# Local attention in twelve whole-unit steps instead of 24 half-unit steps, with the PSUM banks divided anew

## The chip, the core and the metric

The kernel runs on one core of a Trainium2 chip. The metric is the device time of one execution in microseconds (us). The core's engines are TensorE (PE: matmuls and transposes), VectorE (DVE), ScalarE (ACT), GpSimd (POOL) and SyncE (SP), whose queue issues the transfers. PSUM has eight banks, called `bank0` to `bank7` in the program and `bank_251` to `bank_258` in the lists of instructions below.

## What is computed

```python
scores = scale * np.matmul(q, k.transpose(0, 1, 3, 2))          # B=2, H=8, S=768, D=64
is_global = pos[None, :] < int(n_global)                        # 8
is_local = (rel >= 0) & (rel < int(n_local))                    # 96
scores = scores - slopes * dist
scores = np.where(is_global | is_local, scores, -1000000000.0)
a = softmax(scores)
x = np.matmul(a, v)                                             # rearranged to (1536, 512)
g = x @ w_gate
x = (g * sigmoid(g) * (x @ w_val)) @ w_out                      # d_ff 1536
h = x @ w_in                                                    # d_ff 2048
out = (h * np.cos(h)) @ w_out2
```

The reference has its own names for some of these and writes the softmax out, with a maximum subtracted and 1e-9 added to the sum.

## The kernel before

The 1536 rows of q (two batches of 768) form three chunks of four tiles of 128 rows; with four pairs of heads that makes twelve **units**. A tile of queries sees 240 columns of keys (8 global ones and its local window, with one overlap masked), in two blocks of 120; the first tile of a batch sees only 128 (a narrow tile). Units 0 to 3 have a narrow tile in front, units 4 to 7 have one in third place, units 8 to 11 have none.

`attn_fast` (line 571) runs over half units: a group `g` is two tiles and two heads, 24 groups in all (`NG4`), and one step of the loop at line 703 issues pieces of several groups:

- `S_` (604): four score matmuls into two banks of scores; then for each of four tile-heads, on DVE, scores plus distance with a running minimum (L626), and on ACT the exponential with its sum (L629).
- `R_` and `N_` (633, 638): the reciprocals of the sums on DVE (L636), and on POOL the multiplication of P by them (L642).
- `T_` (645): PE transposes P, tile by tile, into a transpose bank (L654), and the bank is copied to `PT` by ACT or DVE (L660). Which one is decided while the program is built: the one whose planned time `self.t` is less.
- `V_` (662): PE multiplies `PT` with v into the bank of results (L676), which holds a whole unit.
- `X_` (679): when a unit is complete, its result is split into a rounded half on ACT (L400) and the rest on DVE (L404).
- `scale` (592): POOL multiplies a unit's q by the factors of its heads (L595). `load` (576): SP fetches q, k, v of a unit two units ahead.

T and V of a group come three steps behind its S (`LAG`). The order on every engine is that in which the program issues the pieces; engines wait for each other by semaphores. Beside this the program converts the weights of the later layers from 64-bit floats (`work`, line 201): ACT lines 198, 209, 221 and DVE lines 218, 224, 233, 236, 240. A planner (`at`, `bg_fill`) puts these operations into gaps of its own estimate of DVE and ACT, up to a goal that grows with the steps (`READY`). The first three conversions write into the buffers in which unit 0's q, k and v lie (`wr_free`).

Behind the attention come two layers (`mlp1`, `mlp2`), whose matmuls are issued at lines 389 to 391.

The banks are given out in `attention` (786): four for scores, two for transposes, two for results. `PTB` and `PB` are the numbers of buffers for transposed and untransposed P.

Of the kernel before, what the change touches and what calls it, by code (L numbers as in the profile page):

```python
# [54 lines left out]
PTB, PB = 6, 20  # L55

NG4, LAG = 24, 3
# [97 lines left out]
class Body:  # L155
# [415 lines left out]
    def attn_fast(self, p, sc, tr, pv):  # L571
# [4 lines left out]
        def load(u):  # L576
# [3 lines left out]
            v = p.tile([128, 8, 128], F32, tag="v", bufs=4, name="v")  # L580
# [17 lines left out]
        def grp(g):  # L598

            u, tp = divmod(g, 2)  # L600
            c, k = units[u]
            return u, c, k, [(t, *_layout(c)[t]) for t in (2 * tp, 2 * tp + 1)]

        def S_(g):

            u, c, k, tiles = grp(g)
            q, kk, _ = op[u]
            bank = [sc(), sc()]
            self.at("pe", sum(t[2] for t in tiles) / 500, (), [id(b) for b in bank])
            for i, (t, off, w, vb) in enumerate(tiles):  # L610
                for h in range(2):
                    a = slice(64 * h, 64 * h + 64)
                    nc.tensor.matmul(bank[h][:, 256 * i:256 * i + w], lhsT=q[a, 128 * t:128 * t + 128],  # L613
                                     rhs=kk[a, off:off + w], start=True, stop=True)
            sums[g] = p.tile([128, 4], F32, tag="sum", bufs=6, name="sum")
            nmins[g] = p.tile([128, 4], F32, tag="nmin", bufs=6, name="nmin")
            for i, (t, off, w, vb) in enumerate(tiles):
                dist = self.base[:, 0:128] if w == 128 else self.base[:, 128:128 + WW]
                for h in range(2):
                    n = 2 * i + h  # L620
                    pt = p.tile([128, WW], F32, tag="P", bufs=PB, name="P")
                    slope = 2.0 ** -(2 * k + h + 1)
                    nm = nmins[g][:, n:n + 1]

                    self.at("d", w / 700, [id(bank[h])], [("P", g, n)])
                    nc.vector.tensor_tensor_reduce(out=pt[:, :w], in0=bank[h][:, 256 * i:256 * i + w], in1=dist,  # L626
                                                   scale=slope, scalar=3.0e38, op0=ALU.add, op1=ALU.min, accum_out=nm)
                    self.at("a", w / 500, [("P", g, n)], [("P", g, n)])
                    nc.scalar.activation(out=pt[:, :w], in_=pt[:, :w], func=AF.Exp, scale=-1.0, bias=nm,  # L629
                                         accum_out=sums[g][:, n:n + 1])  # L630
                    P[g, n] = pt

        def R_(g):
            self.at("d", 0.35, [("P", g, 3)], [("R", g)])
            nc.vector.tensor_scalar_add(sums[g], sums[g], 1.0e-9)
            nc.vector.reciprocal(sums[g], sums[g])  # L636

        def N_(g):
            for i, (t, off, w, vb) in enumerate(grp(g)[3]):
                for n in (2 * i, 2 * i + 1):  # L640
                    self.at("g", w / 400, [("R", g)], [("P", g, n)])
                    nc.gpsimd.tensor_scalar(out=P[g, n][:, :w], in0=P[g, n][:, :w], scalar1=sums[g][:, n:n + 1],  # L642
                                            scalar2=1.0, op0=ALU.mult, op1=ALU.mult)

        def T_(g):

            for i, (t, off, w, vb) in enumerate(grp(g)[3]):
                bank = tr()
                nk, nb = (128, 1) if w == 128 else (KB, 2)
                self.at("pe", 0.11 * 2 * nb, [("P", g, 2 * i), ("P", g, 2 * i + 1)], [id(bank)])  # L650
                for h in range(2):
                    for j in range(nb):
                        o = 128 * (nb * h + j)
                        nc.tensor.transpose(bank[:nk, o:o + 128], P[g, 2 * i + h][:, nk * j:nk * j + nk], self.ident)  # L654
                    del P[g, 2 * i + h]
                pt = ptb[g, i] = p.tile([128, 512], F32, tag="PT", bufs=PTB, name="PT")

                e = "a" if self.t["a"] <= self.t["d"] else "d"
                self.at(e, 0.16 + nb * 0.21, [id(bank)], [("E", g, i)])
                (nc.scalar.copy if e == "a" else nc.vector.tensor_copy)(pt[:nk, :256 * nb], bank[:nk, :256 * nb])  # L660

        def V_(g):

            u, c, k, tiles = grp(g)
            v = op[u][2]
            if g % 2 == 0:
                pvb[u] = pv()
            self.at("pe", 0.25 * sum(len(t[3]) for t in tiles), [("E", g, 0), ("E", g, 1)], [id(pvb[u])])
            for i, (t, off, w, vb) in enumerate(tiles):
                nk = 128 if w == 128 else KB  # L670
                pt = ptb.pop((g, i))
                for j, bl in enumerate(vb):
                    for h in range(2):
                        a = slice(64 * h, 64 * h + 64)
                        o = 128 * (len(vb) * h + j)
                        nc.tensor.matmul(pvb[u][a, 128 * t:128 * t + 128], lhsT=v[:nk, bl, a], rhs=pt[:nk, o:o + 128],  # L676
                                         start=j == 0, stop=j == len(vb) - 1)

        def X_(g):

            u, c, k, _ = grp(g)
            if g % 2 == 0:
                return lambda: None
            xt, ps = self.xtile(c, k), pvb.pop(u)
            self.x[c].append(xt)
            self.split_hi(xt, ps)
            return lambda: self.split_lo(xt, ps)
# [238 lines left out]
```

## Time and profile before

| | |
|---|---|
| median of three runs | 654.55 us (654.12 to 655.04) |
| the profiled execution | 653.59 us |
| its span in the profile | 651.8 us |
| PE busy over the span | 632.7 us (97%) |
| DVE, ACT, POOL busy | 436.1, 391.8, 56.4 us |
| first score matmul of the attention | 9.72 us |
| first matmul of the MLP | 90.70 us |

The span begins with the first and ends with the last instruction that the profile shows; the profiled execution takes 1.8 us more than it. Busy times are sums over an engine's instructions; a busy PE is not PE at its peak, since the ends of matmuls are modelled. The chain that ended last is made of MLP matmuls (lines 389 to 391) for 84% of the span.

### The profile page before, as it was taken

To read this page: it belongs to the slowest core of one execution; us is meant where nothing else is said; L and a number is where in the kernel's file an instruction comes from. 1 tells how busy PE (TensorE), PEld (TensorE's weight loads), DVE (VectorE), ACT (ScalarE), POOL (GpSimd) and SP (SyncE) were. 2 spreads that over 40 slices of the span, in tenths; PEclk is the share of its full clock that TensorE was granted. 3 is DMA by queue.
4 is the path that set the end of the run, shared out by engine and by line. 5 is a ranking of instruction groups with operands and counts; after the bars stand their busy time and mean duration, and the time that the engine had idled before them with its cause. 6 is when DMAs were issued, how large, how long until landed. Compare 5 with 4: busy or idle time off the path is not lost.

```text
span 651.8 us, 8771 instructions
## 1 busy us (share of the span) xinstructions
PE 632.7 (97%) x3176; PEld 516.0 (79%) x3176; DVE 436.1 (67%) x770; ACT 391.8 (60%) x670; POOL 56.4 (9%) x112
## 2 busy tenths in 40 slices
PE   5999989999999999999999999999999999999996
PEld 3776768888888888888888888888888888888885
DVE  4899978877777766438888647866454444544443
ACT  4888776555555544435566349877666666666662
POOL 2677630000000000000000000000000000000000
PEclk9899999999999999999999999999999999999999
DMA  7865246555555455555876643330010000010001
GB/s 259 321 204 199 103 140 227 204 191 200 190 189 196 164 206 195 209 178 193 291 272 240 220 140 98 105 97 25 1 65 1 1 1 1 24 41 0 2 1 69
DMA packets 22803, 88.96 MB, mean 136 GB/s; under 512 B 2656, under 2 KB 4192, under 8 KB 18400
## 3 DMA queue, kind: packets, MB, share of 16 engines
q1 hardware_dynamic: 22320, 88.06, 38.9%
q8 instruction: 27, 0.44, 0.3%
q10 hardware_dynamic: 432, 0.26, 0.1%
q14 instruction: 24, 0.20, 0.1%
HBM read 67.34 MB, written 20.97 MB: 135 GB/s over the span
## 4 chain that ended last, share of the span: by engine, by line
PE 91%; DVE 4%; DMA 2%; issue 0%; ACT 0%; DVEq 0%
PE bank L389 28%; PE bank L391 28%; PE bank L390 28%; PE bank L676 3%; PE bank L613 2%; PE bank L654 2%; DVE P L626 2%; DMA kk<-in_kw 2%; DVE PT L660 1%; DVE x L404 0%; DVE wr L218 0%; DVE sum L636 0%; DVE wr L240 0%; DVE w L224 0%; ACT w L209 0%
## 5 line engine op out<-in xcount | busy, mean ns | idle before, releaser
L389 PE MATMUL bank<-x,w 128*128 128x512 f32 x336 | 131.0, 390 | 0.0
L391 PE MATMUL bank<-x,w 128*128 128x512 f32 x336 | 130.8, 389 | 0.0
L390 PE MATMUL bank<-x,w 128*128 128x512 f32 x336 | 130.8, 389 | 0.0
L481 DVE SCALAR_TENSOR_TENSOR u<-r,bank 128x512 f32<-128x512 f32 x48 | 33.0, 688 | 80.2 <-ACT r L479 80.2
L391 PEld LDWEIGHTS bank<-x,w 128*128 128x128 f32 x336 | 63.1, 188 | 13.1
L389 PEld LDWEIGHTS bank<-x,w 128*128 128x128 f32 x336 | 63.1, 188 | 13.1 <-issue 0.2
L390 PEld LDWEIGHTS bank<-x,w 128*128 128x128 f32 x336 | 63.1, 188 | 13.0
L478 ACT ACTIVATE r<-bank,cst 128x512 f32<-128x512 f32 x48 | 33.0, 687 | 46.0 <-PE bank L391 46.0
L198 ACT ACTIVATE wr<-r 128x1024 f32<-128x1024 f32 x34 | 39.0, 1147 | 29.1 <-DMA r<-in_win 11.7
L391 PE MATMUL bank<-t,w 128*128 128x512 f32 x144 | 56.1, 390 | 0.0
L389 PE MATMUL bank<-t,w 128*128 128x512 f32 x144 | 56.1, 389 | 0.0
L390 PE MATMUL bank<-t,w 128*128 128x512 f32 x144 | 56.1, 389 | 0.0
L629 ACT ACTIVATE P<-P,nmin 128x240 f32<-128x240 f32 (+1 forms) x96 | 44.8, 469 | 13.4 <-DVE nmin L626 13.4
L491 DVE TENSOR_TENSOR r<-bank,r 128x512 f32<-128x512 f32 x48 | 33.1, 689 | 28.4 <-ACT r L490 28.4
L489 ACT ACTIVATE r<-r 128x512 f32<-128x512 f32 x48 | 30.4, 633 | 33.8 <-DVE r L482 33.6
L642 POOL TENSOR_SCALAR P<-P,sum 128x240 f32<-128x240 f32 (+1 forms) x96 | 48.1, 519 | 21.7 <-DVE sum L636 7.8
L425 ACT ACTIVATE e<-bank 128x512 f32<-128x512 f32 x36 | 21.4, 595 | 46.0 <-PE bank L391 44.3
L391 PE MATMUL bank<-big,g 128*128 128x512 f32 x120 | 46.8, 390 | 0.0
L389 PE MATMUL bank<-big,g 128*128 128x512 f32 x120 | 46.7, 390 | 0.0
L390 PE MATMUL bank<-x,big 128*128 128x512 f32 x120 | 46.7, 389 | 0.0
L390 PE MATMUL bank<-big,g 128*128 128x512 f32 x120 | 46.7, 389 | 0.0
L389 PE MATMUL bank<-x,big 128*128 128x512 f32 x120 | 46.7, 389 | 0.0
(95 smaller groups left out, 1237.0 us busy)
## 6 DMA issues: line engine op xcount, KB each, us to landing
scr<-wr SPq DMA_DIRECT2D x34, 512.0 KB, 2.9
r<-in_wo SPq DMA_DIRECT2D x14, 1024.0 KB, 5.8
r<-in_gv SPq DMA_DIRECT2D x12, 1024.0 KB, 5.9
wl<-scr SPq DMA_DIRECT2D x18, 512.0 KB, 5.0
r<-in_win SPq DMA_DIRECT2D x8, 1024.0 KB, 6.0
wr<-scr SPq DMA_DIRECT2D x16, 512.0 KB, 3.4
v<-in_vw SPq DMA_DIRECT2D x11, 512.0 KB, 5.5
out<-wr SPq DMA_DIRECT2D x11, 256.0 KB, 2.4
```

Source lines behind the costliest of these rows:

```text
L198: self.nc.scalar.activation(out=w, in_=self.raw[n][:, :, 1].bitcast(F32), func=AF.Abs)
L389: mm(out, lhsT=ah, rhs=bh, start=first, stop=False)
L390: mm(out, lhsT=ah, rhs=bl, start=False, stop=False)
L391: mm(out, lhsT=al, rhs=bh, start=False, stop=last)
L425: nc.scalar.activation(out=tmp, in_=ps[0], func=AF.Silu)
L478: nc.scalar.activation(out=r, in_=h, func=AF.Identity, scale=INV2PI, bias=self.magic)
L481: nc.vector.scalar_tensor_tensor(out=u, in0=r, scalar=-C1, in1=h, op0=ALU.mult, op1=ALU.add)
L489: nc.scalar.activation(out=r, in_=r, func=AF.Abs)
L491: nc.vector.tensor_tensor(out=r, in0=h, in1=r, op=ALU.mult)
L629: nc.scalar.activation(out=pt[:, :w], in_=pt[:, :w], func=AF.Exp, scale=-1.0, bias=nm, accum_out=sums[g][:, n:n + 1])
L642: nc.gpsimd.tensor_scalar(out=P[g, n][:, :w], in0=P[g, n][:, :w], scalar1=sums[g][:, n:n + 1], scalar2=1.0, op0=ALU.mult, op1=ALU.mult)
L676: nc.tensor.matmul(pvb[u][a, 128 * t:128 * t + 128], lhsT=v[:nk, bl, a], rhs=pt[:nk, o:o + 128], start=j == 0, stop=j == len(vb) - 1)
```

## The change

A step now issues pieces of whole units: four tiles and two heads, eight score matmuls into all four banks of scores. There are twelve steps (`NU`) and T and V lag two of them. Three banks serve the transposes, and one the results. A unit's reciprocals and normalisations are issued in two halves (`R_(u, i)`): the first behind the S of the unit, the second among the DVE operations of the next unit's S. `scale` and `load` are called once a step, `X_` as one piece at a step's start. v has five buffers for four, PT eight for six, P 24 for 20. `wr_free` is raised a step earlier or later by the new count of steps, and the goal grows with the new steps.

```diff
-PTB, PB = 6, 20
+PTB, PB = 8, 24
-NG4, LAG = 24, 3
+NU, LAG = 12, 2
...
-        def S_(g):
-            u, c, k, tiles = grp(g)
-            bank = [sc(), sc()]
+        def S_(u):
+            c, k, tiles = grp(u)
+            bank = [[sc(), sc()] for _ in range(2)]
+            for i in range(2):
+                self.at("pe", sum(t[2] for t in tiles[2 * i:2 * i + 2]) / 560, (), [id(b) for b in bank[i]])
+                for t, off, w, vb in tiles[2 * i:2 * i + 2]:
+                    for h in range(2):
+                        a = slice(64 * h, 64 * h + 64)
+                        nc.tensor.matmul(bank[i][h][:, 256 * (t % 2):256 * (t % 2) + w],
+                                         lhsT=q[a, 128 * t:128 * t + 128], rhs=kk[a, off:off + w],
+                                         start=True, stop=True)
+            for t, off, w, vb in tiles:
+                if t == 2 and u:
+                    R_(u - 1, 1)
...
+        def R_(u, i):
+            self.at("d", 0.35, [("P", u, 4 * i + 3)], [("R", u, i)])
+            h = sums[u][:, 4 * i:4 * i + 4]
+            nc.vector.tensor_scalar_add(h, h, 1.0e-9)
+            nc.vector.reciprocal(h, h)
+            for t, off, w, vb in grp(u)[2][2 * i:2 * i + 2]:
+                for n in (2 * t, 2 * t + 1):
+                    self.at("g", w / 400, [("R", u, i)], [("P", u, n)])
+                    nc.gpsimd.tensor_scalar(out=P[u, n][:, :w], in0=P[u, n][:, :w], scalar1=sums[u][:, n:n + 1],
...
-        def T_(g):
-            for i, (t, off, w, vb) in enumerate(grp(g)[3]):
+        def T_(u):
+            for t, off, w, vb in grp(u)[2]:
                 bank = tr()
...
-        for s in range(NG4 + LAG + 1):
-            self.wr_free = 3 if s > 1 + LAG else 2 if s > 1 else 0
-            low = X_(s - LAG - 1) if s > LAG else None
-            if LAG <= s < NG4 + LAG:
+        for s in range(NU + LAG + 1):
+            self.wr_free = 3 if s > LAG else 2 if s > 0 else 0
+            if s > LAG:
+                X_(s - LAG - 1)
+            if LAG <= s < NU + LAG:
                 T_(s - LAG)
-            if s < NG4:
-                if s % 2 == 1 and s // 2 + 1 < len(units):
-                    scale(s // 2 + 1)
+            if s < NU:
+                if s + 1 < len(units):
+                    scale(s + 1)
                 S_(s)
-            if 1 <= s <= NG4:
-                R_(s - 1)
-                N_(s - 1)
-            if low:
-                low()
-            if LAG <= s < NG4 + LAG:
+                R_(s, 0)
+            elif s == NU:
+                R_(s - 1, 1)
+            if LAG <= s < NU + LAG:
                 V_(s - LAG)
-            if s % 2 == 0 and s // 2 + 2 < len(units):
-                load(s // 2 + 2)
+            if s + 2 < len(units):
+                load(s + 2)
             yield s
...
-        for s in self.attn_fast(p, Rot([banks[i] for i in (0, 1, 6, 7)]), Rot(banks[2:4]), Rot(banks[4:6])):
-            self.filling, self.goal = True, READY * s / NG4
+        for s in self.attn_fast(p, Rot([banks[i] for i in (0, 1, 6, 7)]), Rot(banks[2:5]), Rot(banks[5:6])):
+            self.filling, self.goal = True, READY * s / NU
```

The lists below are the instructions of one engine in the order of the program. First ACT in the attention's second half, where the units are wide: `P` rows are exponentials, `x` rows the rounded half of the split, `PT` rows copies out of transpose banks, `wr` a weight conversion. Before:

```order
L629 ACTIVATE P,sum<-P,nmin 128x240 x8
L400 CAST x_1184<-bank_256 128x512
L629 ACTIVATE P,sum<-P,nmin 128x240 x4
L660 COPY PT<-bank_254 120x512
L629 ACTIVATE P,sum<-P,nmin 128x240 x4
L400 CAST x_1276<-bank_255 128x512
L629 ACTIVATE P,sum<-P,nmin 128x240 x4
L660 COPY PT<-bank_254 120x512
```

With the change:

```order
L634 ACTIVATE P,sum<-P,nmin 128x240 x8
L400 CAST x_1097<-bank_256 128x512
L665 COPY PT<-bank_254 120x512
L665 COPY PT<-bank_255 120x512
L665 COPY PT<-bank_254 120x512
L198 ACTIVATE wr_84<-r_817 128x1024
L634 ACTIVATE P,sum<-P,nmin 128x240 x8
L400 CAST x_1193<-bank_256 128x512
```

The exponentials of a whole unit now stand in a row, and a split and three of a unit's four copies stand behind them; in the same stretch of the list before there is one copy or split to four exponentials.

PE in the same part of the program: `P` rows are transposes into a transpose bank, `kk` rows scores, `PT` rows results. Before:

```order
L676 MATMUL bank_255<-PT,v 64x128 x8
L654 MATMUL bank_253<-cst,P 120x128 x4
L654 MATMUL bank_254<-cst,P 120x128 x4
L613 MATMUL bank_252<-kk,q 128x240
L613 MATMUL bank_257<-kk,q 128x240
L613 MATMUL bank_252<-kk,q 128x240
L613 MATMUL bank_257<-kk,q 128x240
L676 MATMUL bank_255<-PT,v 64x128 x8
```

With the change:

```order
L679 MATMUL bank_256<-PT,v 64x128 x16
L659 MATMUL bank_253<-cst,P 120x128 x4
L659 MATMUL bank_254<-cst,P 120x128 x4
L659 MATMUL bank_255<-cst,P 120x128 x4
L659 MATMUL bank_253<-cst,P 120x128 x4
L615 MATMUL bank_252<-kk,q 128x240
L615 MATMUL bank_257<-kk,q 128x240
```

A unit's four tiles now go through three banks in a row: the fourth writes the bank of the first (253 here), and the scores stand behind it.

POOL at the start of the program: `wr_82` is the q of unit 0, the `q` rows are the scalings of units 1 and 2, `P` rows normalisations. Before:

```order
L595 TENSOR_SCALAR wr_82<-wr_82,cst 128x512
L595 TENSOR_SCALAR q<-q,cst 128x512
L642 TENSOR_SCALAR P<-P,sum 128x128 x2
L642 TENSOR_SCALAR P<-P,sum 128x240 x6
L595 TENSOR_SCALAR q<-q,cst 128x512
```

With the change:

```order
L595 TENSOR_SCALAR wr_82<-wr_82,cst 128x512
L595 TENSOR_SCALAR q<-q,cst 128x512
L647 TENSOR_SCALAR P<-P,sum 128x128 x2
L647 TENSOR_SCALAR P<-P,sum 128x240 x2
L595 TENSOR_SCALAR q<-q,cst 128x512
L647 TENSOR_SCALAR P<-P,sum 128x240 x4
```

The scaling of unit 2 has moved ahead of the second four normalisations of unit 0.

## Rows read from the trace of the kernel before

**Rows 1.** Windows: us; busy of PE, PEld, DVE, ACT, POOL; PEclk; DMA share; GB/s.
```profile
20.20:75.60 55.40, 53.14 (x534) 38.83 (x534) 52.79 (x222) 45.74 (x163) 39.78 (x81) 1.00 0.63 214
...
90.70:640.00 549.30, 549.30 (x2425) 455.09 (x2424) 356.61 (x458) 323.19 (x442) 0.00 (x0) 1.00 0.36 127
```

**Rows 2.** Timeline of PE: start us, us, engine, line, operation, out<-in, shapes.
```profile
14.02 1.66 PE L654 MATMUL bank<-cst,P 128*128 128x128 f32 x6 [1.25 <-POOL P L642]
...
20.24 0.90 PE L613 MATMUL bank<-kk,q 64*128 64x128 f32 x8 [0.16 <-DMA kk<-in_kw]
...
66.37 1.08 PE L613 MATMUL bank<-kk,q 64*128 64x240 f32 x8
67.38 1.09 PE L676 MATMUL bank<-PT,v 120*64 120x128 f32 x16
68.41 1.09 PE L654 MATMUL bank<-cst,P 128*120 128x128 f32 x8
69.43 1.08 PE L613 MATMUL bank<-kk,q 64*128 64x240 f32 x8
...
75.61 1.08 PE L613 MATMUL bank<-kk,q 64*128 64x240 f32 x8
...
89.54 1.23 PE L676 MATMUL bank<-PT,v 120*64 120x128 f32 x16 [0.28 <-ACT PT L660]
90.70 0.50 PE L389 MATMUL bank<-x,w 128*128 128x512 f32 x1
```

**Rows 3.** Timeline of DVE, the same columns: first minimum operations of a step.
```profile
21.14 0.29 DVE L626 CUSTOM_DVE_ANT_0 P<-bank,base 128x128 f32<-128x128 f32 x1 [0.33 <-PE bank L613]
...
70.65 0.41 DVE L626 CUSTOM_DVE_ANT_0 P<-bank,base 128x240 f32<-128x240 f32 x1 [0.19 <-PE bank L613]
```

**Rows 4.** Timeline of ACT: exponentials, a split, a conversion, a copy.
```profile
21.48 0.40 ACT L629 ACTIVATE P<-P,nmin 128x128 f32<-128x128 f32 x1 [1.02 <-DVE nmin L626]
...
23.22 0.56 ACT L400 CAST x<-bank 128x512 fp32r<-128x512 f32 x1
...
23.69 1.18 ACT L221 ACTIVATE se<-r 128x1024 int32<-128x1024 uint32 x1
...
24.75 0.51 ACT L629 ACTIVATE P<-P,nmin 128x240 f32<-128x240 f32 x1
...
71.10 0.49 ACT L629 ACTIVATE P<-P,nmin 128x240 f32<-128x240 f32 x1 [0.57 <-DVE nmin L626]
...
88.91 0.58 ACT L660 COPY PT<-bank 120x512 f32<-120x512 f32 x1
```

**Rows 5.** Groups by shape, 9 to 91 us: count | busy us, mean ns | idle.
```profile
L629 ACT ACTIVATE P<-P,nmin 128x240 f32<-128x240 f32 x80 | 38.5, 484 | 8.6 <-DVE nmin L626 8.6
...
L660 DVE COPY PT<-bank 120x512 f32<-120x512 f32 x31 | 20.6, 681 | 2.1 <-PE bank L654 2.0
...
L629 ACT ACTIVATE P<-P,nmin 128x128 f32<-128x128 f32 x16 | 6.3, 394 | 4.8 <-DVE nmin L626 4.8
...
L660 ACT COPY PT<-bank 120x512 f32<-120x512 f32 x9 | 5.1, 572 | 0.6 <-PE bank L654 0.6
...
L236 DVE SCALAR_TENSOR_TENSOR wr<-r,wr 128x1024 int32<-128x1024 int32 x2 | 2.4, 1222 | 0.0
...
L660 ACT COPY PT<-bank 128x256 f32<-128x256 f32 x3 | 1.0, 348 | 0.0
```

**Rows 6.** Timeline of POOL: normalisations and a scaling.
```profile
15.59 1.78 POOL L642 TENSOR_SCALAR P<-P,sum 128x240 f32<-128x240 f32 x4 [0.40 <-ACT P L629]
19.38 0.69 POOL L595 TENSOR_SCALAR q<-q,cst 128x512 f32<-128x512 f32 x1 [2.01 <-DMA q<-in_qT]
...
78.72 3.00 POOL L642 TENSOR_SCALAR P<-P,sum 128x240 f32<-128x240 f32 x4 [0.98 <-PE bank L654]
```

**Rows 7.** Windows of a microsecond at the start, columns as in rows 1.
```profile
13.00:14.00 1.00, 0.00 (x0) 0.00 (x0) 0.97 (x9) 1.00 (x5) 0.41 (x2) 1.00 1.02 381
...
17.00:18.00 1.00, 1.00 (x12) 1.00 (x12) 1.00 (x7) 0.60 (x3) 0.37 (x1) 0.50 1.00 400
```

More of the change, by code (lines that the diff above doesn't have):

```diff
@@ L596, in scale, with grp @@
                                     op0=ALU.mult, op1=ALU.mult)
-        def grp(g):
-            u, tp = divmod(g, 2)
+        def grp(u):
             c, k = units[u]
-            return u, c, k, [(t, *_layout(c)[t]) for t in (2 * tp, 2 * tp + 1)]
-        def S_(g):
-            u, c, k, tiles = grp(g)
+            return c, k, [(t, *_layout(c)[t]) for t in range(4)]
+        def S_(u):
+            c, k, tiles = grp(u)
             q, kk, _ = op[u]
-            bank = [sc(), sc()]
[L609 to L617, printed above, removed]
+            bank = [[sc(), sc()] for _ in range(2)]
+            sums[u] = p.tile([128, 8], F32, tag="sum", bufs=4, name="sum")
+            nmins[u] = p.tile([128, 8], F32, tag="nmin", bufs=4, name="nmin")
+            for i in range(2):
[9 more added lines that the diff above has]
+                    R_(u - 1, 1)
@@ L631, in S_ @@
[L631 to L638, printed above, removed]
-            for i, (t, off, w, vb) in enumerate(grp(g)[3]):
-                for n in (2 * i, 2 * i + 1):
-                    self.at("g", w / 400, [("R", g)], [("P", g, n)])
-                    nc.gpsimd.tensor_scalar(out=P[g, n][:, :w], in0=P[g, n][:, :w], scalar1=sums[g][:, n:n + 1],
+                                         accum_out=sums[u][:, n:n + 1])
@@ L653, in T_, with V_ @@
                         o = 128 * (nb * h + j)
-                        nc.tensor.transpose(bank[:nk, o:o + 128], P[g, 2 * i + h][:, nk * j:nk * j + nk], self.ident)
-                    del P[g, 2 * i + h]
-                pt = ptb[g, i] = p.tile([128, 512], F32, tag="PT", bufs=PTB, name="PT")
+                        nc.tensor.transpose(bank[:nk, o:o + 128], P[u, 2 * t + h][:, nk * j:nk * j + nk], self.ident)
+                    del P[u, 2 * t + h]
+                pt = ptb[u, t] = p.tile([128, 512], F32, tag="PT", bufs=PTB, name="PT")
                 e = "a" if self.t["a"] <= self.t["d"] else "d"
-                self.at(e, 0.16 + nb * 0.21, [id(bank)], [("E", g, i)])
+                self.at(e, 0.16 + nb * 0.21, [id(bank)], [("E", u, t)])
                 (nc.scalar.copy if e == "a" else nc.vector.tensor_copy)(pt[:nk, :256 * nb], bank[:nk, :256 * nb])
-        def V_(g):
-            u, c, k, tiles = grp(g)
+        def V_(u):
             v = op[u][2]
[L666 to L669, printed above, removed]
+            out = pvb[u] = pv()
+            for t, off, w, vb in grp(u)[2]:
+                self.at("pe", 0.22 * len(vb), [("E", u, t)], [id(out)])
                 nk = 128 if w == 128 else KB
-                pt = ptb.pop((g, i))
+                pt = ptb.pop((u, t))
                 for j, bl in enumerate(vb):
@@ L675, in V_, with X_ @@
                         o = 128 * (len(vb) * h + j)
[L676 removed]
+                        nc.tensor.matmul(out[a, 128 * t:128 * t + 128], lhsT=v[:nk, bl, a], rhs=pt[:nk, o:o + 128],
                                          start=j == 0, stop=j == len(vb) - 1)
[L679 to L684, printed above, removed]
+        def X_(u):
+            c, k = units[u]
+            xt = self.xtile(c, k)
             self.x[c].append(xt)
[L686 to L687 removed]
+            self.split_out(xt, pvb.pop(u))
         op[0] = self.pro.q, self.pro.k, self.pro.v
```

18 lines of the change are left out of this document (9 added, 9 removed).

## The prediction

> **What bounds the kernel now.** I read the windows first. From 90.70 us on TensorE (PE) is busy for all 549.30 us of the window that ends at 640 [rows 1]; nothing there waits, and the change touches no line that runs there. So the end moves by as much as the first MLP matmul, now at 90.70 us, moves [rows 2]. The attention is the part ahead of it. Between the first score matmul of unit 2 (20.24 us) and that of unit 11 (75.61 us) PE is busy 53.14 of 55.40 us and VectorE (DVE) 52.79, ScalarE (ACT) 45.74 [rows 1]: PE and DVE are both nearly full, ACT has a sixth free. The PE timeline shows the undisturbed pattern: scores, results and transposes of half a unit take 1.01, 1.03 and 1.02 us, so 3.06 us a half step, 6.1 a unit [rows 2].
>
> I call a step's pieces as the code does: S the eight score matmuls, T the transposes (tile 0 to 3), V the results, X the two halves of the split. E0 to E3 are the copies of the four transposed tiles out of their banks.
>
> **The copies move to ACT.** Before, ACT's queue mixes one split or one copy with each four exponentials, and most copies are DVE's. In the changed order ACT has, in every step from the fourth on, eight exponentials, then the split of the unit three steps back, then E0, E1 and E3; DVE has E2 alone. DVE is relieved by more than 20 copies, which I cost at nothing: it no longer sets the pace. PE meanwhile has three transpose banks for four tiles. Tile 3 writes the bank of tile 0, so it waits for E0; S of the unit follows tile 3 in PE's queue; and E0 stands on ACT behind the exponentials of the previous unit. That closes a ring of waits, which I price for one step, from S(k) to S(k+1), all four tiles wide:
>
> - S starting to the first bias-and-minimum on DVE: 70.65 - 69.43 = 1.22 us, DVE idle until PE released it [rows 2, 3].
> - that one to the first exponential: 71.10 - 70.65 = 0.45 [rows 3, 4].
> - eight exponentials of 0.48 each, back to back: 3.84 [rows 5].
> - the split, 23.22 to 23.69: 0.47 [rows 4].
> - E0: 0.57 [rows 5], and 0.05 to PE, as the copy that starts at 88.91 and takes 0.58 lets V go at 89.54 [rows 2, 4]: 0.62.
> - tile 3's transposes, half of 69.43 - 68.41: 0.51 [rows 2].
>
> The sum is 7.11 us, against 6.1 of PE work: PE idles a microsecond in each step. E1, E3 and a background conversion fit into the time in which ACT waits for the next scores.
>
> Units whose first tile is narrow (0 to 3) have 21.14 - 20.24 = 0.90 and 21.48 - 21.14 = 0.34 at the start [rows 2, 3], six exponentials of 0.48 and two of 0.39 (3.66), and a narrow E0 of 0.35 + 0.05 [rows 5]: 6.28. Units 4 to 7 have their narrow tile third: 1.67 + 3.66 + 0.47 + 0.62 + 0.51 = 6.93, but 6.71 from S(4) to S(5), since that E0 is unit 3's. From S(2) to S(11) that is 2 x 6.28 + 6.71 + 3 x 6.93 + 3 x 7.11 = 61.4 us. Before it is 55.37 [rows 2]. **Loop: +6.0.**
>
> **Background work in the loop.** An ACT conversion steps 24.75 - 23.69 = 1.06 us [rows 4]; E3 is over 0.6 us after S has started and the first exponential comes 1.67 after it, so it just fits: nothing. If that gap were missed, it costs 1.06 at each of seven places, which I keep for the upper end. On DVE a step's list in the ring is the second half of the split, E2, and the first minimum, which the scores release at 7.11 + 1.22 = 8.3 us after the previous S. The first half of the split is over at 6.0; the second half and E2 take 0.68 each [rows 5], to 7.4; a conversion of 1.22 behind them [rows 5] makes that 8.6, 0.3 too late. This stands once in the changed list, in step 9, with two more conversions ahead of the split, so I take 0.4; one more stands among the minimum operations of step 4, where the exponentials have used up less than its length by then: 0.3. **+0.7** (between 0, all in slack, and 2.4, two at full length).
>
> **The start.** GpSimd (POOL) scales q of unit 2 when its transfer lands, at 19.38 us, having waited for it [rows 6]. Before, all eight normalisations of unit 0 stand ahead of that scaling and are done by 17.37. Now only four do: the scaling moves ahead of the other four, which start at 19.38 + 0.69 = 20.07 and take 1.78, to 21.85. Transposes of tiles 2 and 3 of unit 0 wait for them, and S(2) behind those starts at 21.85 + 0.05 + 0.25 = 22.15, not 20.24. SP's queue has the same transfers in the same order here, so q lands when it did. **+1.9** (0 if q lands earlier, 3 if later). Unit 3's scaling is past that: no wait stands in front of it before, and its transfer is issued as early.
>
> PE then does nothing from about 15.6, where the first two tiles' transposes give way to the next piece now [rows 2], to 20.6 us. In the run before the granted clock was 0.50 (1.2 GHz) from 17 to 18, after a stretch with PE at 0.00 busy from 13 to 14 [rows 7]. I expect the lower level behind the longer gap too: tile 3's last transposes, the first scores and the results of unit 0 take up to twice as long, of which the ring sees some **+0.4** (0 to 1.5).
>
> **The end.** Behind S(11) the last exponential is over at 1.67 + 3.84 = 5.51, E0 of unit 10 at 6.55, tile 3 at 7.11, V(10) at 9.15. The last normalisations come behind a DVE copy, at 7.7, and beside a two-operand conversion take 3.00, as at 78.72 [rows 6]: 10.8. Tile 3 of unit 11 follows to 11.3, V(11) to 13.35. Before it was 90.70 - 75.61 = 15.09 [rows 2]. **-1.7** (-3 to 0).
>
> **Nothing** I cost: the wider sums and minima buffers; the fifth v and the 24 P buffers, whose readers are two steps back; one result bank instead of two, since T and S of a step lie between the split that reads it and the V that writes it again. The later release of the third scratch buffer and the planner's new goal leave DVE's list at the last split a few conversions further on than before, so the first MLP weights are no later. If they were late, PE would wait in the MLP; nothing there is idle now.
>
> **Sum:** 1.9 + 0.4 + 6.0 + 0.7 - 1.7 = +7.3 us on the profiled execution's 653.59, so 660.9. That execution is 0.96 under the median of the three runs, 654.55; I leave the number as the sum gives it, and the range covers that difference.
>
> **Rivals.**
>
> *The copies are hidden (faster).* Three banks let tiles 0 to 2 go while E0 runs. If E0 ended before tile 2's transposes do, PE would never wait and a step would be its work. In a step tile 2 ends 2.03 (S) + 2.04 (V) + 1.53 = 5.6 us after the previous S; E0 ends at 1.67 + 3.84 + 0.47 + 0.57 = 6.55. It decides only if eight exponentials took under 2.9 us, 0.36 each, where rows show 0.48 [rows 5], or if ACT's list were taken out of order. PE's own work from S(2) to S(11), with the narrow tiles, is 50.6 us: 55.4 - 50.6 = -4.8, with the start's +1.9 and the end's -1.7 this is 649.0. The Trainium skill, "Perfetto Trace Analysis", section "Optimizing Tensor Performance", says that independent matmul groups should rotate through banks so that the evacuation of one overlaps the next group's matmuls. By that rule a third transpose bank gives this rival's time; against it stands what occupies ACT in the rows. 5%.
>
> *Only start and end change.* The ring is there, but its extra microsecond a step lies in waits that the loop has already (DVE's 95% share speaks for some of that): +1.9 + 0.4 - 1.7, 654.2. Before has PE idle only 2.3 us in the loop, which speaks against it. 4%.
>
> *The conversions do not fit.* E3 waits for tile 3, so a conversion can push the exponentials by its whole length: 7 x 1.06 = 7.4 more, 668.3. ACT waits 0.57 us before its first exponential in the row at 71.10, less than a conversion [rows 4]. 8%.
>
> **How the numbers follow.** The ring has 83%. Its own terms, with the ends above, go from 657 to 665. The range goes to 656 and 666: below lie the hidden copies and the start-and-end case (9%), above the conversions (8%), so little more than 17% is out. A measurement can tell about 0.2% here, 1.3 us: faster 6% (the first rival and a little), same 4%, slower 90%.
>
> **What would show it.** S matmuls of units 8 to 11 start 7.1 us apart, not 6.1. The idle time before the transposes is put down to ACT's PT copy, in a gap of about 1 us once a step; ACT busy over 90% in the loop and DVE under 85%. S(2) starts near 22 us, behind transposes that wait for POOL, and POOL for the transfer of q. The first MLP matmul comes near 98 us and the stretch behind it stays 549 us. Wrong would be: steps of 6.1 us and no idle time before tile 3 (then the evacuation is hidden), S(2) still at 20.2, or new waits in the MLP.

## The result, and the profile after

The changed kernel takes 663.94 us (median of four runs, 662.83 to 664.11) against 654.66 us for the kernel before on the same chip: 1.0139 times as long, with a 95% interval of 1.0126 to 1.0152. The prediction was 660.9 us in a range of 656 to 666, with a chance of 0.90 for slower. The profiled execution took 663.83 us, 10.24 more than that of before.

The windows of the changed kernel, columns as in [rows 1], cut where its stages now end: up to the scores of unit 2, the loop to those of unit 11, the end of the attention, the MLP.

```profile
9.95:23.05 13.10, 8.06 (x47) 5.35 (x46) 7.63 (x42) 8.39 (x33) 4.93 (x12) 0.81 0.99 384
23.05:87.63 64.58, 52.37 (x531) 42.80 (x531) 47.88 (x207) 56.76 (x185) 43.72 (x84) 0.93 0.56 189
87.63:100.92 13.29, 11.83 (x146) 10.01 (x145) 10.79 (x32) 11.91 (x28) 7.07 (x12) 1.00 0.02 4
100.92:650.20 549.28, 549.28 (x2425) 454.85 (x2424) 354.35 (x455) 321.37 (x441) 0.00 (x0) 1.00 0.36 125
```

The MLP is untouched: 549.28 us, PE busy throughout, against 549.30 [rows 1]. It starts 10.22 us later (100.92 for 90.70), and this is all of the difference: start +2.81 (23.05 for 20.24), loop +9.21 (64.58 for 55.37), end -1.80 (13.29 for 15.09) [rows 2]. In the loop PE's busy time hardly changed and DVE's fell by 5 us, but ACT's rose by 11 and the loop grew around it.

PE's timeline, columns as in [rows 2]: the start, the last two steps of the loop (scores of units 9, 10 and 11), the first MLP matmul.

```profile
21.12 2.00 PE L659 MATMUL bank<-cst,P 128*120 128x128 f32 x8 [4.67 <-POOL P L647]
23.05 2.53 PE L615 MATMUL bank<-kk,q 64*128 64x128 f32 x16
...
72.37 3.43 PE L615 MATMUL bank<-kk,q 64*128 64x240 f32 x16
...
79.82 0.62 PE L659 MATMUL bank<-cst,P 128*120 128x128 f32 x4 [0.78 <-POOL P L647]
80.37 1.89 PE L615 MATMUL bank<-kk,q 64*128 64x240 f32 x16
...
87.08 0.62 PE L659 MATMUL bank<-cst,P 128*120 128x128 f32 x4 [1.46 <-POOL P L647]
87.63 1.89 PE L615 MATMUL bank<-kk,q 64*128 64x240 f32 x16
...
100.92 0.50 PE L389 MATMUL bank<-x,w 128*128 128x512 f32 x1
```

DVE and then ACT in the same steps: the conversion and the first minimum of step 9, the first minimum of step 10; on ACT the first and last of step 10's exponentials, then the split, E0 and E1 in one row, E3, and behind it a conversion and the next exponential.

```profile
72.32 1.35 DVE L236 SCALAR_TENSOR_TENSOR wr<-r,wr 128x1024 int32<-128x1024 int32 x1
74.34 0.41 DVE L631 CUSTOM_DVE_ANT_0 P<-bank,base 128x240 f32<-128x240 f32 x1 [0.67 <-PE bank L615]
...
81.59 0.41 DVE L631 CUSTOM_DVE_ANT_0 P<-bank,base 128x240 f32<-128x240 f32 x1 [1.08 <-PE bank L615]
```

```profile
82.04 0.50 ACT L634 ACTIVATE P<-P,nmin 128x240 f32<-128x240 f32 x1 [0.93 <-DVE nmin L631]
...
85.41 0.48 ACT L634 ACTIVATE P<-P,nmin 128x240 f32<-128x240 f32 x1
...
85.89 0.56 ACT L400 CAST x<-bank 128x512 fp32r<-128x512 f32 x1
86.35 1.06 ACT L665 COPY PT<-bank 120x512 f32<-120x512 f32 x2
87.79 0.58 ACT L665 COPY PT<-bank 120x512 f32<-120x512 f32 x1 [0.38 <-PE bank L659]
88.27 1.05 ACT L209 CAST w<-wr 128x1024 fp32r<-128x1024 f32 x1
89.30 0.50 ACT L634 ACTIVATE P<-P,nmin 128x240 f32<-128x240 f32 x1
```

The ring can be read off piece by piece from 80.37 to 87.63: scores to first minimum 1.22, to the first exponential 0.45, eight exponentials 3.85, the split 0.46, E0's start to tile 3 0.73, tile 3 to the next scores 0.55. That is the whole 7.26 us of a step. But the row of tile 3 names POOL's normalisation as its releaser, and so does most of this wait in the list of waits from 23 to 90 us (engine and line, what it waited for: us in total, times, longest):

```profile
PE bank L659 <- POOL P L647: 7.8, 6, 1.9
...
PE bank L659 <- ACT PT L665: 4.4, 3, 1.9
```

Tile 3 waits for two things, its own normalised P and the bank that E0 empties. POOL's timeline, up to the tile 3 that starts at 87.08:

```profile
83.45 3.56 POOL L647 TENSOR_SCALAR P<-P,sum 128x240 f32<-128x240 f32 x8 [2.08 <-DVE sum L643]
```

By the program's order the first four of these eight are unit 9's and the last four unit 10's, and this tile 3 is unit 9's. Its normalisations were over half way through the row, at 85.2, while E0, 0.58 long, was over at 86.93, 0.15 before tile 3. The label goes by POOL's last event ahead of that start, the end of the row at 87.01, which is unit 10's. Counted in the same way, tile 3 follows the end of E0 by 0.14 or 0.15 us in all nine steps of the loop, and in eight of them its own P had been ready for 1.5 to 2.0 us (in the step that ends with the scores of unit 5 for 0.08). The experiments test this. **Theory A** is the prediction's: the copy of tile 0, behind the exponentials and the split in ACT's queue. **Theory B** is the label's: POOL.

### The profile page after: what moved, and what is told of

Its sections match the earlier page's. It is cut to its first block, busy times and chain, and to the rows that moved or that the text cites. A ratio compares the mean times of both kernels' runs of the same rounds, so it can differ in the third digit from the quotient of the medians.

```text
span 662.0 us, 8783 instructions
## 1 busy us (share of the span) xinstructions
PE 631.1 (95%) x3176; PEld 519.9 (79%) x3176; DVE 426.0 (64%) x748; ACT 401.5 (61%) x692; POOL 57.1 (9%) x112
## 4 chain that ended last, share of the span: by engine, by line
PE 92%; ACT 2%; POOL 2%; issue 2%; DVE 1%; DVEq 1%; POOLq 0%; ACTq 0%
PE bank L391 28%; PE bank L389 28%; PE bank L390 28%; PE bank L615 3%; PE bank L659 2%; PE bank L679 2%; POOL P L647 2%; ACT P L634 2%; DVEq L845 1%; DVE P L631 1%; PE bank L698 1%; ACT PT L665 0%; ACT x L400 0%; ACT w L209 0%; DVEq L853 0%
## 5 line engine op out<-in xcount | busy, mean ns | idle before, releaser
L391 PE MATMUL bank<-big,g 128*128 128x512 f32 x120 | 46.8, 390 | 0.0
L389 PE MATMUL bank<-big,g 128*128 128x512 f32 x120 | 46.7, 389 | 0.0
L389 PE MATMUL bank<-x,big 128*128 128x512 f32 x120 | 46.7, 389 | 0.0
L390 PE MATMUL bank<-x,big 128*128 128x512 f32 x120 | 46.7, 389 | 0.0
L391 PE MATMUL bank<-x,big 128*128 128x512 f32 x120 | 46.7, 389 | 0.0
```

The source lines that it names most:

```text
L389: mm(out, lhsT=ah, rhs=bh, start=first, stop=False)
L390: mm(out, lhsT=ah, rhs=bl, start=False, stop=False)
L391: mm(out, lhsT=al, rhs=bh, start=False, stop=last)
```

## The experiments

Ratios are to the kernel before, run on the same chip beside each.

**1. The split out of the ring.** X is called between tile 0's transposes and tile 1's; each copy keeps its engine.

```diff
-        def T_(u):
+        def T_(u, mid=lambda: None):
...
             for t, off, w, vb in grp(u)[2]:
+                if t == 1:
+                    mid()
                 bank = tr()
...
-                e = "a" if self.t["a"] <= self.t["d"] else "d"
+                e = "d" if t == 2 or (u == 0 and t < 2) else "a"
...
-            if s > LAG:
-                X_(s - LAG - 1)
+            mid = (lambda: X_(s - LAG - 1)) if s > LAG else (lambda: None)
...
-                T_(s - LAG)
+                T_(s - LAG, mid)
```

> The changed kernel with the split of the next results called between the transposes of tile 0 and those of tile 1, so that ScalarE's order in each step is exps, copy of tile 0, split half, copies of tiles 1 and 3, while every copy stays on the engine that it has in the changed kernel. Theory A (ScalarE's copy of tile 0, which stands behind all exps and the split half, opens the bank that tile 3 needs): the split half of 0.47 us leaves the loop in each of nine steps, so the spacing of the scores falls from 7.26 to about 6.8 us and the time from 663.9 to about 659.7 us (658.5 to 661). Theory B (the last event of that wait, POOL's normalisation, is what tile 3 waits for): POOL's work stands where it stood, spacing 7.26, time 663.5 to 664.5 us.

Measured: 661.3 us, 1.0109 (1.0092 to 1.0126). PE's timeline, two quiet steps, and DVE's in a later one:

```profile
42.43 1.71 PE L615 MATMUL bank<-kk,q 64*128 64x240 f32 x16
...
49.04 1.71 PE L615 MATMUL bank<-kk,q 64*128 64x240 f32 x16
...
55.63 1.71 PE L615 MATMUL bank<-kk,q 64*128 64x240 f32 x16
```

```profile
77.21 1.28 DVE L236 SCALAR_TENSOR_TENSOR wr<-r,wr 128x1024 int32<-128x1024 int32 x1
...
79.62 0.39 DVE L631 CUSTOM_DVE_ANT_0 P<-bank,base 128x240 f32<-128x240 f32 x1
```

Steps of 6.61 and 6.59 us, where the changed kernel has 7.09 and 7.08: the split's 0.47 has left the ring, as A says, and B's "no change" is wrong. The time fell by less than expected, because three later steps were long (7.32, 7.68 and 7.75 us). In the last, scores that started at 77.41 got their first minimum 2.21 us later instead of 1.22, behind a conversion, the split's second half and a copy on DVE; the step of 7.68 had its scores at half speed (3.24 us at 62.95). The time lies 0.3 us above A's range.

**2. The copy of tile 0 made later.** E0 and E2 change engines; on DVE E0 stands behind the split's second half.

```diff
-                e = "a" if self.t["a"] <= self.t["d"] else "d"
+                e = "d" if t == 0 else "a"
```

> The changed kernel with one edit: the copy of tile 0 goes to VectorE, that of tile 2 to ScalarE; the split stays ahead of the transposes, so the copy of tile 0 stands on VectorE behind the split's second half, which itself waits for ScalarE's first half. Theory A: the copy comes later by the second half (about 0.84 us) in each of nine steps, so the spacing goes from 7.26 to about 8.1 us and the time to about 671 us (668 to 673). Theory B (POOL's normalisation is what tile 3 waits for): 663 to 665 us.

Measured: 674.85 us, 1.0312 (1.0295 to 1.0329). PE's timeline:

```profile
62.08 1.71 PE L615 MATMUL bank<-kk,q 64*128 64x240 f32 x16
...
69.44 0.62 PE L659 MATMUL bank<-cst,P 128*120 128x128 f32 x4 [2.73 <-DVE PT L665]
69.99 3.51 PE L615 MATMUL bank<-kk,q 64*128 64x240 f32 x16
```

A step of 7.91 us, 0.80 more than the same one in the changed kernel, and the wait is now put down to the copy on DVE; POOL's work is what it was. A holds for the step, and moving the copy to another queue is no gain by itself. The time is 1.9 us above A's range: three steps with scores at half speed, the one shown at 69.99 us among them, took 8.4 to 8.9 us.

**3. The copy of tile 0 made early.** E0 and E2 on DVE, and the split's second half behind the copies.

```diff
-                e = "a" if self.t["a"] <= self.t["d"] else "d"
+                e = "d" if t % 2 == 0 else "a"
...
-            self.split_out(xt, pvb.pop(u))
+            ps = pvb.pop(u)
+            self.split_hi(xt, ps)
+            return lambda: self.split_lo(xt, ps)
...
-            if s > LAG:
-                X_(s - LAG - 1)
+            low = X_(s - LAG - 1) if s > LAG else None
             if LAG <= s < NU + LAG:
                 T_(s - LAG)
+            if low:
+                low()
```

> The changed kernel with the copy of tile 0 (and of tile 2) on VectorE and the split's second half behind all copies on that engine, the first half ahead of them on ScalarE as before: the copy that opens tile 3's bank now stands behind no exp at all. Theory A: the wait of tile 3 goes, TensorE's work of 6.1 us becomes the bound of a wide step, the loop falls from 64.6 to 55 to 57 us and the time to 654.5 to 656.5 us. Theory B (POOL's normalisation): the normalisations stand where they stood and the time stays at 663 to 665 us. A third way, that ScalarE's own work per step is the bound (88% busy in the loop), would leave 6.4 us a step or more and a time of 657 us or more.

Measured: 658.71 us, 1.0066 (1.0049 to 1.0083). PE's timeline:

```profile
67.32 1.89 PE L615 MATMUL bank<-kk,q 64*128 64x240 f32 x16
...
72.72 0.62 PE L659 MATMUL bank<-cst,P 128*120 128x128 f32 x4 [0.37 <-POOL P L647]
73.27 1.89 PE L615 MATMUL bank<-kk,q 64*128 64x240 f32 x16
...
88.11 3.61 PE L679 MATMUL bank<-PT,v 120*64 120x128 f32 x32 [1.64 <-DVE x L404]
```

The step is 5.95 us, the next and last one too, and the loop 56.56, inside A's 55 to 57: with E0 behind no exponential the ring is gone. (The other steps took 5.3 to 7.2 us, the longest with its scores at half speed. Tile 3 still follows E0, now by DVE's queue, with 0.37 us of idle time here.) The time, 658.71, is above A's range. It lies where the third way put it, but that way's step of 6.4 us or more is not there: the edit's own cost came at the end. Results of the last units waited for the late half of the split (1.64 and 0.75 us), those behind the first wait ran at half speed (3.61 us for 1.97), and from the last scores to the MLP it took 17.24 us instead of 13.29.

**4. Without normalisation.**

```diff
-                    self.at("g", w / 400, [("R", u, i)], [("P", u, n)])
-                    nc.gpsimd.tensor_scalar(out=P[u, n][:, :w], in0=P[u, n][:, :w], scalar1=sums[u][:, n:n + 1],
-                                            scalar2=1.0, op0=ALU.mult, op1=ALU.mult)
+                    pass
```

> The changed kernel without POOL's normalisation: the multiplication of the exps by the reciprocal sums is left out, so the attention's weights are not normalised; everything else stands. Theory A: in the wide steps the spacing stays 7.26 us, because the copy of tile 0 on ScalarE still comes last; only the first unit's transposes come earlier (they stand behind POOL's second half there), worth 2.5 to 4 us: 660 to 661.5 us. Theory B: the wait goes in every step, the spacing falls to about 6.1 us and the time to 651 to 654 us.

Measured: 660.2 us, 1.0101 (1.0084 to 1.0118). PE's timeline and the list of waits from 23 to 90 us:

```profile
54.47 1.71 PE L615 MATMUL bank<-kk,q 64*128 64x240 f32 x16
...
60.78 0.65 PE L657 MATMUL bank<-cst,P 128*120 128x128 f32 x4 [1.68 <-ACT PT L663]
61.36 1.89 PE L615 MATMUL bank<-kk,q 64*128 64x240 f32 x16
```

```profile
PE bank L657 <- ACT PT L663: 15.8, 10, 1.8
```

POOL is out of it, yet the wait is there, ten times in the window, and this step takes 6.89 us, where the changed kernel's takes 7.11. This settles it for A: what carried POOL's label is a wait for the copy on ACT. The spacing is not quite the 7.26 us that A expected: 7.21, 7.21 and 7.09 us from the scores of unit 8 to those of unit 11. In the profiled execution the start gave 2.8 us of the gain, as A had it (the scores of unit 2 start at 20.23 us instead of 23.05), and the loop 1.9 (62.64 us for 64.58).

**5. The start, first try.** All scalings behind the normalisations of their step.

```diff
-                if s + 1 < len(units):
-                    scale(s + 1)
                 S_(s)
                 R_(s, 0)
+                if s + 1 < len(units):
+                    scale(s + 1)
```

> The changed kernel with one call moved: the scaling of the next step's queries on POOL stands behind the step's normalisations instead of ahead of them. Theory A (at the start POOL waits 3.97 us for the queries' transfer with the second half of unit 0's normalisations behind it, and TensorE's transposes wait 4.7 us for those): the scores of unit 2 start at about 20.7 us instead of 23.05, the half-speed stretch of TensorE behind that wait goes with it, and the time falls by 2 to 3 us, to about 661.3 us (660.3 to 662.3); the spacing of later steps stays at 7.1 to 7.3 us. Theory B (the start is bound by the transfers themselves, the queries' and keys' landing): under 0.5 us, 663.4 to 664.4 us. A third way: in later steps the scaling now ends behind the normalisations and the scores wait for it, which would make the loop longer and the time 664 us or more.

Measured: 672.7 us, 1.028 (1.0264 to 1.0295): the third way, and more. PE's timeline, scores of units 1 and 5:

```profile
16.61 3.20 PE L615 MATMUL bank<-kk,q 64*128 64x128 f32 x16 [4.48 <-POOL q L595]
...
46.61 3.20 PE L615 MATMUL bank<-kk,q 64*128 64x240 f32 x16 [1.80 <-POOL q L595]
```

Unit 1's scaling, too, had moved behind four normalisations; its scores started at 16.61 us instead of 12.37, and later scores waited for scalings again. The edit tested more than the start. Two larger versions carried the same flaw: the copies of run 3 with this scaling and the end's results in free banks of scores took 672.04 us, and with earlier reciprocals 670.85. Neither tells anything of what it was meant for.

> Three edits of the changed kernel together: the copies of tiles 0 and 2 on VectorE with the split's second half behind them (as in the run before that had 658.7 us), the scaling of the queries behind the normalisations, and the results of the last two units in banks of the scores, which are free by then, so that the end no longer waits for the split of the one result bank. Theory A: the start gives 2 to 2.5 us, the end 3 to 4 us (17.24 to about 13.5 us from the last scores to the first matmul of the MLP), the loop stays at 56 to 57 us: 651.5 to 654 us, about equal to the kernel before. If TensorE's waits for POOL's normalisations (9.6 us of idle time in that run) grow when TensorE comes earlier, the gains are eaten: 655 to 657 us.

> The same three edits and a fourth: the reciprocals of the previous unit's second half stand on VectorE behind two of the step's eight minima instead of behind four, so that POOL normalises that half about 0.7 us earlier. Theory A (with the copy of tile 0 out of ScalarE's queue, the wait of tile 3 is now really one for POOL's normalisations, 9.6 us in the run with the copies moved): 1 to 3 us less than with three edits, 649 to 652 us, which beats the kernel before. Theory B (ScalarE's or TensorE's own work bounds the step by then): within 0.7 us of the version with three edits.

**6. The start alone.** Only unit 2's scaling moves, between the two halves that it had parted.

```diff
                 if t == 2 and u:
                     R_(u - 1, 1)
+                    if u == 1:
+                        scale(2)
...
-                if s + 1 < len(units):
+                if s + 1 < len(units) and s != 1:
                     scale(s + 1)
```

> The changed kernel with one call of one step moved: the scaling of unit 2's queries stands on POOL behind the second half of unit 0's normalisations and ahead of unit 1's first half; every other scaling stands where it stands in the changed kernel. Theory A: the scores of unit 2 start at 20.6 to 21.0 us instead of 23.05, and the half-speed stretch of TensorE after that wait, which made the first interval 7.15 us, goes or shrinks; the time falls by 2 to 3 us, to 660.9 to 662 us. Theory B (the start is bound by the transfers): 663.4 to 664.4 us.

Measured: 661.5 us, 1.0113 (1.0092 to 1.0134). PE's timeline:

```profile
20.55 3.20 PE L615 MATMUL bank<-kk,q 64*128 64x128 f32 x16 [0.68 <-POOL q L595]
...
28.10 1.71 PE L615 MATMUL bank<-kk,q 64*128 64x128 f32 x16
```

The scores of unit 2 start 2.50 us earlier. The half-speed stretch did not go, though: the first interval is 7.55 us for 7.15. In the time the gain is small: 1.0113 for the changed kernel's 1.0139, two intervals that just overlap.

**7. The banks alone, on the steps of before.**

```diff
-        for s in self.attn_fast(p, Rot([banks[i] for i in (0, 1, 6, 7)]), Rot(banks[2:4]), Rot(banks[4:6])):
+        for s in self.attn_fast(p, Rot([banks[i] for i in (0, 1, 6, 7)]), Rot(banks[2:5]), Rot(banks[5:6])):
```

> The kernel before with its steps of half a unit kept and only the banks dealt as in the changed kernel: three for transposes, one for results, instead of two and two. Theory A (the steps of a whole unit, with four tiles of transposes in one go, make the new wait): half a unit's two tiles never need a bank that the same step filled, so the time stays within 2 us of the kernel before: 653.5 to 656 us. Theory B (the single bank for results, which the next unit's results have to wait for, is what costs): 658 to 664 us.

Measured: 684.14 us, 1.0454 (1.0438 to 1.047). Theory A's number is far off; B's cause is right, but its range of 658 to 664 us is far off too. PE's timeline and DVE's:

```profile
27.00 1.55 PE L676 MATMUL bank<-PT,v 128*64 128x128 f32 x12 [2.46 <-DVE x L404]
```

```profile
26.28 0.66 DVE L404 TENSOR_TENSOR x<-bank,x 128x512 fp32r<-128x512 f32 x1
```

Once a unit the results wait some 2.5 us for the split to empty the one bank (22.3 us in nine waits). In the kernel before the split's second half is issued behind the scores of its step, so it stands on DVE behind their minimum operations. The changed kernel issues the whole split ahead of the transposes and scores, and its loop shows no idle time before the results. That this order is why one bank does there is argued from the two programs: no run put the second half behind the minima in steps of whole units.

**8. The steps alone, on the banks of before.** The reverse edit, on the changed kernel.

> The changed kernel with its steps of a whole unit kept and only the banks dealt as in the kernel before: two for transposes, two for results. Theory A (the ring through the copies and the transposes' banks sets the step): tile 2 now waits for the copy of tile 0 and tile 3 for that of tile 1, so one more tile's transposes of about 0.5 us stand between the copies and the scores; the spacing of wide steps goes from 7.1 to 7.3 to about 7.7 us, the time to 668 us (666 to 671). Theory B (the single bank for results is what costs, as it is in the half-unit steps, where that deal alone took 684.1 us): faster than the changed kernel, 655 to 661 us.

Measured: 670.68 us, 1.0245 (1.0228 to 1.0263). PE's timeline:

```profile
67.96 1.89 PE L615 MATMUL bank<-kk,q 64*128 64x240 f32 x16
...
74.66 1.10 PE L659 MATMUL bank<-cst,P 128*128 128x128 f32 x6 [2.10 <-ACT PT L665]
75.69 3.39 PE L615 MATMUL bank<-kk,q 64*128 64x240 f32 x16
```

A step of 7.73 us, 0.47 more than with three banks: one more tile behind the copies, as A says. So each half of the change alone costs more than both together: the banks 30.0 us, the steps 16.9, both 9.3.

**9. What was lost, put back.** The copies of run 3, the start of run 6, and the last two units' results in free banks of scores; then the same with reciprocals behind two minima instead of four.

```diff
-            out = pvb[u] = pv()
+            out = pvb[u] = sc() if u >= NU - 2 else pv()
```

> Three edits of the changed kernel: the copies of tiles 0 and 2 on VectorE with the split's second half behind them (658.7 us alone), the scaling of unit 2's queries between unit 0's second half and unit 1's first half, and the results of the last two units in banks of the scores. Theory A: start minus 2 to 2.5 us, end minus 2.5 to 3.5 us against the run with the copies alone: 653 to 654.5 us, about equal to the kernel before. If what bounds the step by then is POOL's normalisations, for which TensorE had waited 9.6 us in that run, the start's gain comes back as such waits: 655 to 656.5 us.

> The same three edits and the reciprocals of the previous unit's second half behind two minima of the step instead of four, so that POOL normalises that half about 0.7 us earlier. If TensorE's waits for POOL bound the step: 1 to 3 us less than with three edits, 650.5 to 653 us, which beats the kernel before (654.2). If ScalarE's or TensorE's own work bounds it: within 0.7 us of the version with three edits.

Measured: 653.93 us, 0.9997 (0.9988 to 1.0007), and 653.78 us, 0.9998 (0.9986 to 1.0010): both equal to the kernel before. PE's timeline of the first, scores of units 2 and 11 and the MLP:

```profile
20.34 3.20 PE L615 MATMUL bank<-kk,q 64*128 64x128 f32 x16 [1.96 <-DMA kk<-in_kw]
...
76.52 1.89 PE L615 MATMUL bank<-kk,q 64*128 64x240 f32 x16
...
91.19 0.50 PE L389 MATMUL bank<-x,w 128*128 128x512 f32 x1
```

Against run 3 the start gave 2.3 us (20.34 for 22.66) and the end 2.6 (14.67 for 17.24); the loop stayed at 56.18. So whole-unit steps cost nothing once the copies, unit 2's scaling and the last results stand elsewhere, and they gain nothing either. With the earlier reciprocals the MLP began at 89.67 us in the profile, 1.5 earlier, but the medians are 0.15 apart: no gain that can be measured. About 0.5 of the 1.5 came back as a wait in the MLP, for a converted weight (line 391 behind DVE's line 224), which the run without them does not have. So the waits that carry POOL's label did not bound the step there either.

## Why the prediction was right, point by point

**The ring** is there, in the place and with the pieces that the prediction gave, and it is most of the loss. Its size was low by 0.15 in a wide step: 7.26 us for 7.11. The pieces that differ are E0 to tile 3 (0.73 for 0.62) and tile 3 to the scores (0.55 for 0.51).

| interval of scores | predicted | measured |
|---|---|---|
| units 2-3 | 6.28 | 7.15 |
| 3-4 | 6.28 | 6.56 |
| 4-5 | 6.71 | 7.07 |
| 5-6, 6-7, 7-8 | 6.93 each | 7.09, 7.08, 7.11 |
| 8-9, 9-10, 10-11 | 7.11 each | 7.26, 8.00, 7.26 |

The sum is 64.58 for 61.4. Of the 3.2 between them, about 1.6 is the ring's pieces, 0.15 to 0.28 in each of nine steps. About 1.3 is the clock: 0.6 in the first interval, where the first minimum came 1.63 us after the scores started and a step later 1.04, and 0.74 in the one of 8.00. The remaining 0.2 is the conversion in step 4, below.

**The background work** (+0.7) was put in the wrong place. Of the 0.3 for the conversion among the minima of step 4, 0.2 can be seen. The 0.4 for step 9 cannot: its conversion ended at 73.67 us, and DVE then idled 0.67 until PE's slow scores released the minimum at 74.34. At full speed the minimum would have been due at 73.59 (72.37 + 1.22), so the conversion would have cost 0.08. The price of 0.68 for the split's second half stands in no row of [rows 5]; it measured 0.69 (86.48 us). A conversion on ACT just fits behind E3, as predicted: it ends at 89.32, and the exponential starts at 89.30.

**The clock** (+0.4, at the start alone) was the term sized worst. At the start it fell as expected, to 0.50 from about 17.9 to 24.8 us, and the 0.6 of the first interval with the 0.35 ahead of it (next paragraph) lies within the 0 to 1.5 allowed. But it fell twice more inside the loop, for which there was no term. Windows of a microsecond, columns as in [rows 1]:

```profile
60.00:61.00 1.00, 1.00 (x10) 0.71 (x10) 0.97 (x8) 1.00 (x5) 0.00 (x0) 0.50 0.66 266
...
71.00:72.00 1.00, 0.18 (x2) 0.21 (x3) 1.00 (x3) 1.00 (x3) 1.00 (x2) 1.00 0.79 307
...
73.00:74.00 1.00, 1.00 (x8) 0.83 (x7) 0.67 (x1) 1.00 (x2) 1.00 (x2) 0.50 0.06 16
```

After a PE that was nearly idle, 0.50 (1.2 GHz) was granted from about 72.6 to 76.0 us (worked out from the means of the windows at its ends, 0.78 and 0.52, as the other times here), so the scores at 72.37 took 3.43 us instead of 1.89 and the first minimum came 1.97 us after they started instead of 1.22. The earlier fall, from about 58.9 to 62.3 us, cost the ring nothing: it caught the results behind the scores (2.72 us for 1.75), and the step took 7.11. The prediction had PE idle a microsecond in each step and did not ask what the clock would do with that.

**The start** (+1.9) was +2.81. The mechanism was right (POOL's timeline):

```profile
19.94 0.69 POOL L595 TENSOR_SCALAR q<-q,cst 128x512 f32<-128x512 f32 x1 [3.97 <-DMA q<-in_qT]
20.60 3.78 POOL L647 TENSOR_SCALAR P<-P,sum 128x240 f32<-128x240 f32 x8
```

The scaling came at 19.94 for 19.38 us [rows 6], since q landed 0.56 later, and the transposes behind it took 2.00 us at half speed, which made the scores another 0.35 late. Run 6 takes this term away by moving one call, and the scores come at 20.55.

**The end** (-1.7) was -1.80, and by the steps that the prediction gave. Counted from the scores of unit 11, the results of unit 10 were over after 9.2 us (9.15 predicted), the last normalisations ran from 7.9 to 11.0 (7.7 to 10.8, though 7.7 and 3.00 make 10.7), and the MLP began after 13.29 (13.35). POOL's row:

```profile
95.51 3.09 POOL L647 TENSOR_SCALAR P<-P,sum 128x240 f32<-128x240 f32 x4 [0.79 <-DVE sum L643]
```

**Nothing**, for the single result bank, holds in the changed order: no results wait in its loop. The prediction's reason, that T and S lie between the split and V, is not the whole of it. In run 7 they lie between the split's first half and V as well, but its second half stands behind the minima, and one bank cost 30 us; what the shorter steps add to that was not tried.

**The rival of hidden copies** fell. The prediction weighed the Trainium skill, "Perfetto Trace Analysis", "Optimizing Tensor Performance", where groups that rotate through banks overlap their evacuation. The runs bear it out as far as a bank goes: the third one is worth 0.47 us a step (run 8), but four tiles in three banks still wait for a copy, and the copy's place in its queue decides how long (runs 1 to 3). Of the other two, *only start and end change* fell with the loop's +9.21 us, and *the conversions do not fit* with the one that ends at 89.32 beside an exponential that starts on time.

**The signs** that the text named were there but three: ACT was busy 88% of the loop (56.76 of 64.58 us) where it said over 90, the wait was mostly labelled POOL, and the MLP began at 100.92 us, 2.9 later than the 98 that it named.

**The sum** was +7.3 us against +10.2 in the profiled executions. Of the 2.9 missing, the ring's size makes 1.6, the clock 1.3 (0.6 and 0.74 in the loop and 0.35 at the start, less the 0.4 that was allowed), the later q 0.6; the background work gives 0.5 back and the end 0.1.

## What to carry to other kernels

When a step is made coarser, follow the last bank that it fills back to the copy that empties it, and count what stands ahead of that copy in its engine's queue; a copy behind a long run of exponentials closes a ring. Moving the copy to a place in another queue with nothing long ahead of it opened the ring again (7.26 to 5.95 us in the loop's last step); a place behind the split's second half made it longer (7.11 to 7.91). A buffer saved in one place may rest on an order elsewhere: one result bank shows no wait with the split issued early, and cost 30 us in half-unit steps with its second half issued late. Where a wait has two releasers, count in the program's order which instruction of each it needs, or take one of them away, before believing the label.

## What the runs showed of the hardware

- The releaser named for a wait can be the wrong one of two: 7.8 us were put down to POOL, and with POOL's work gone the same waits were put down to ACT and lasted about as long (ahead of unit 9's scores 1.82 us for 1.89). The event that was named ahead of unit 11's scores belonged to another unit's normalisation (87.01 us, where the ones that were needed were over at 85.2).
- Without POOL's work two pieces of the ring were shorter by a tenth: E0's start to tile 3 took 0.63 us (53.25 to 53.88) for 0.73, and scores to first minimum 1.11 (54.47 to 55.58) for 1.22. In the changed kernel the queues hold wait instructions of their own ahead of these two, nine of 51 ns for PE's line 659 and 34 of 21 ns for DVE's line 631 from 23 to 90 us; without POOL's work they hold none. By their length that is 0.05 of the first tenth and 0.02 of the second. The rest is open: no run separated POOL's activity from the second semaphore that tile 3 no longer waits for.
- The granted clock fell to 0.50 in some steps behind PE's idle time and not in others: it was 1.00 over the whole loop in the profile without normalisation, where PE idled 1.3 to 1.8 us a step, and 0.93 in the changed kernel's, with up to 1.9. Executions of one program differ in it too: over the whole span the one profiled without normalisation had a mean of 0.998, the other three 0.989 to 0.991. What decides it was not tried.
